# Four layers of multi-query attention: VectorE builds its exps inside their own tile, and the written order of the instructions is replaced

## The chip, the cores and the metric

The kernel runs on one core of a Trainium2 chip. The metric is the device time of one execution in microseconds (us), as the median of several runs. The engines are named as in the profile: PE is TensorE (matmuls), DVE is VectorE, ACT is ScalarE, POOL is GpSimd, SP is SyncE, which here issues the DMAs.

## What is computed

Two sets of weights, A and B, are used in turn for four attention layers over a sequence of 2048 rows of width 512. There are 32 query heads of width 16 and a single key and value head that they all share. Cut to what matters, the reference is:

```python
def layer(x, wq, wk, wv, wo):                # S = 2048, D = 512, H = 32, Dh = 16
    q = (x @ wq).reshape(B, S, H, Dh).transpose(0, 2, 1, 3)
    k = x @ wk
    v = x @ wv
    p = softmax(einsum("bhqd,bkd->bhqk", q, k) * Dh ** -0.5)
    o = einsum("bhqk,bkd->bhqd", p, v)
    return o.transpose(0, 2, 1, 3).reshape(B, S, H * Dh) @ wo

for w in (A, B, A, B):
    x = x + layer(layernorm(x), *w)
```

Each layer has 32 x 2048 x 2048 exponentials, 134 million. They are the bulk of the elementwise work, and they are shared between two engines.

## The kernel before, in words

**Units of work.** A layer is cut into 4 blocks of 512 queries and 4 groups of 8 heads, so there are 16 pairs (block, group) in a layer. For a pair, the 2048 keys are taken in 32 chunks of 64, and each chunk in two *halves*. One half is a tile of scores of 128 partitions x 1024 elements, so there are 4096 halves in the four layers. Each half goes through three steps: PE multiplies queries by keys (the score), one of two engines takes the exp and writes it as float32 into one of 16 slots of the tile `pt`, and PE multiplies the exps by the values and accumulates in `acc`. A column of ones in the value tile gives the sum of the exps in the same matmul, so the division comes at the end of a pair.

**Who takes the exp.** For most halves PE writes the scores into one of two PSUM tiles `st` (function `score`, L746), and ACT reads the whole 128x1024 with one ACTIVATE (L756). For the others PE writes the scores into one PSUM bank, `by_v`, in two parts of 512 (`score_v`, L761), and DVE makes the exp by arithmetic (`exp_first`, L778, and `chain`, L808). That takes eight DVE instructions: two TENSOR_SCALAR (L785), one for each part, scale the score and add a constant, and their int32 output holds the exponent and the fraction of the power of two; one TENSOR_SCALAR (L800) cuts out the fraction into the tile `mant`; one (L802) masks the exponent; three SCALAR_TENSOR_TENSOR (L794) evaluate a polynomial in `mant`; and a fourth (L794 again, reading `e`) multiplies by the exponent's power. The int32 values lie in a tile `e` of which there are two, `e0` and `e1`, taken in turn; the polynomial is evaluated in the slot of `pt` itself. DVE takes its halves 24 halves ahead of ACT (`AHEAD`), so that its longer chain is done when PE needs the exp.

**What else DVE does.** It evacuates every other product from PSUM (queries, keys, values, outputs), does the layer norm, and collects and divides the sums of each pair.

**The other products.** Queries, keys, values and output products of the layers use the PSUM bank `beside`. PE's array is used as two independent halves of 64 rows: a step of the order gives each half of the array one or two groups of four matmuls of 64x32.

**The order.** Nothing schedules at run time or at build time: the string `ORDER` (L55 to L194) is the order of all engines' work, one letter for each step. What matters here: `S` is a score for ACT together with its ACTIVATE; `a` is one value matmul group on each half of the array; `b`, `c`, `d`, `e` put a value group beside product groups; `f` to `k`, `r`, `s` carry a score part for DVE; `P` and `F` are steps that use the whole array; `I` is one L785 of DVE; `0` and `1` are the next instruction of the older and of the younger of at most two DVE chains; `X` is the next DVE step of the products; `G` and `D` evacuate and divide sums; `Y` is a one-element copy (L860) that makes DVE wait for the steps so far; `Q` loads queries by DMA. Each engine runs its instructions in this order, and semaphores hold an instruction until its data are there. PE in particular runs in order: a score that waits holds everything behind it.

**Layer boundaries.** The keys of a new layer come block by block from the outputs of the old one. The new layer's first three pairs take the keys of blocks 0 to 2 first and block 3 afterwards, which gives the last block's chain (output products, layer norm, transposes, key product, the five DVE instructions that begin with `vf`, L578, and end with `kop`, L395) some time. A score that reads block 3's `kop` waits for that chain.

**Waits.** The framework gives each instruction the semaphore waits that its tiles need. When an instruction needs more than one, the others stand before it as instructions of their own (EVENT_SEMAPHORE in the profile). `declare_no_dep` takes a dependence out between two named instructions; it is used where a slot of `pt` is written again, since PE's reads in between order the two writers already.

## Time and profile before

| what | value |
|---|---|
| median of 3 runs | 3555.32 us (3551.79 to 3559.22) |
| the profiled execution's own time | 3529.43 us |
| its span, first to last instruction | 3527.6 us |
| mean granted TensorE clock | 0.994 |
| busy: PE, ACT, DVE | 97%, 97%, 93% of the span |

All durations below come from the profiled execution, which is 25.9 us (0.7%) shorter than the median of the timed runs. In the profile, a group's row gives the instruction's line, engine, operation, output and inputs, the count, the busy time in us and the mean duration in ns, then the idle time of that engine just before them and who ended it. A busy time is the union of the durations. The durations of consecutive instructions on DVE and on ACT overlap, so what an instruction costs its engine is the distance from its start to the next one's start, and not its duration. In the timeline, rows are start, length, engine, line and operation; equal instructions in succession are merged, with `xN` and the length of all.

### The profile page before, as it was taken

How to read it: one execution, taken by the hardware profiler on the slowest of the kernel's cores; microseconds unless marked ns; L12 is line 12 of the kernel's file. 1: busy time of each engine (PE TensorE's matmuls, PEld its weight loads, DVE VectorE, ACT ScalarE, POOL GpSimd, SP SyncE). 2: the span in 40 equal slices, each digit the busy share in tenths (PEclk: the TensorE clock that was granted, in tenths of full speed). 3: DMA queues.
4: the chain of work that ended last, by engine and by line, in shares of the span. 5: the costliest groups of instructions: out<-in, count | busy, mean ns of one | idle time of the engine just before them, and what ended most of it. 6: DMA issues, size and time to landing. Idle time of an engine off the chain costs nothing.

```text
span 3527.6 us, 234143 instructions
## 1 busy us (share of the span) xinstructions
PE 3424.3 (97%) x111859; PEld 2162.8 (61%) x111859; DVE 3288.6 (93%) x4417; ACT 3429.4 (97%) x3728; POOL 158.8 (5%) x110
## 2 busy tenths in 40 slices
PE   7999999999999999999999999999999999999997
PEld 4666666665666666666566666665656666665653
DVE  4869999999989999999998999999999999999994
ACT  6999999999999999999999999999999999999996
POOL 1000001000000000000000010000000010000000
PEclk9999999999999999999999999999999999999999
DMA  2121111111012111011111111101101111111110
GB/s 93 64 74 45 43 42 33 32 40 46 27 43 63 32 43 48 27 49 36 31 31 60 48 45 50 33 31 39 50 23 37 54 43 35 45 34 40 32 33 20
DMA packets 91837, 149.56 MB, mean 42 GB/s; under 512 B 28985, under 2 KB 45369, under 8 KB 90873
## 3 DMA queue, kind: packets, MB, share of 16 engines
q1 hardware_dynamic: 90872, 134.49, 12.0%
q8 instruction: 876, 14.35, 1.6%
q14 instruction: 89, 0.72, 0.1%
HBM read 90.57 MB, written 34.59 MB: 35 GB/s over the span
## 4 chain that ended last, share of the span: by engine, by line
PE 44%; ACT 43%; DVE 11%; DMA 1%; issue 1%; SPq 0%; POOL 0%; DVEq 0%; ACTq 0%; POOLq 0%
ACT pt L756 43%; PE acc L475 23%; PE st L475 12%; PE beside L475 6%; DVE pt L794 5%; DVE e L785 1%; PE by_v L475 1%; DVE mant L800 1%; DVE e L802 1%; PE beside L372 1%; PE beside L512 1%; DMA rec<-rs 0%; DVE sum L877 0%; SPq L913 0%; DMA qt<-qs 0%
## 5 line engine op out<-in xcount | busy, mean ns | idle before, releaser
L756 ACT ACTIVATE pt<-st 128x1024 f32<-128x1024 f32 x3722 | 3425.2, 1118 | 46.0 <-PE st L475 41.2
L475 PE MATMUL acc<-pt,vop 64*32 64x256 f32 x65536 | 2830.9, 377 | 6.1 <-issue 3.7
L475 PE MATMUL st<-qt,kop 64*32 64x512 f16 x29776 | 1654.3, 381 | 55.1 <-ACT pt L756 36.4
L475 PEld LDWEIGHTS acc<-pt,vop 64*32 64x32 f32 x65536 | 1460.8, 106 | 364.7 <-issue 19.3
L475 PEld LDWEIGHTS <-kop 64*32 64x32 f16 x32768 | 771.3, 90 | 806.2 <-issue 514.8
L794 DVE SCALAR_TENSOR_TENSOR pt<-pt,mant 128x1024 f32<-128x1024 f32 x748 | 913.5, 1221 | 3.7
L785 DVE TENSOR_SCALAR e<-by_v 128x512 int32<-128x512 f32 x748 | 514.0, 687 | 61.2 <-PE by_v L475 33.6
L794 DVE SCALAR_TENSOR_TENSOR pt<-pt,e 128x1024 f32<-128x1024 f32 x374 | 458.6, 1226 | 0.8
L475 PE MATMUL beside<-xnT,wq 64*32 64x512 f16 x5952 | 456.8, 376 | 2.0 <-DVE gv L415 1.1
L794 DVE SCALAR_TENSOR_TENSOR pt<-mant 128x1024 f32<-128x1024 f32 x374 | 455.4, 1218 | 0.0
L475 PE MATMUL beside<-wo,ot 64*32 64x512 f16 x5664 | 432.1, 376 | 4.7 <-issue 2.4
L475 PE MATMUL by_v<-qt,kop 64*32 64x512 f16 x2992 | 298.7, 377 | 2.9 <-DVE e L785 1.5
L802 DVE TENSOR_SCALAR e<-e 128x1024 int32<-128x1024 int32 x374 | 256.7, 686 | 3.2
L800 DVE TENSOR_SCALAR mant<-e 128x1024 int32<-128x1024 int32 x374 | 257.4, 688 | 1.0
L475 PEld LDWEIGHTS <-wq 64*32 64x32 f16 x5952 | 172.4, 92 | 49.3 <-issue 7.9
L475 PEld LDWEIGHTS <-ot 64*32 64x32 f16 x5664 | 163.9, 92 | 49.8 <-issue 10.3
L423 POOL TENSOR_TENSOR sq<-qs 128x512 bf16<-128x512 f16 x64 | 107.9, 1686 | 1066.6 <-DVE qs L420 1066.6
L877 DVE COPY sum<-acc 128x512 f32<-128x512 f32 x128 | 84.4, 682 | 39.4 <-PE acc L475 39.0
L475 PE MATMUL beside<-xnT,wkv 64*32 64x512 f16 x1440 | 107.7, 376 | 0.0
L359 POOL TENSOR_TENSOR rstd<-var,nhalf 128x4 f32<-128x4 f32 x16 | 25.9, 1621 | 1126.5 <-DVE var L358 1126.5
L420 DVE TENSOR_SCALAR qs<-beside 128x512 f16<-128x512 f32 x63 | 43.1, 684 | 25.8 <-PE beside L475 13.3
L448 DVE SCALAR_TENSOR_TENSOR xt<-beside,xt 128x512 f32<-128x512 f32 x64 | 43.8, 684 | 12.3 <-PE beside L512 11.1
(105 smaller groups left out, 755.2 us busy)
## 6 DMA issues: line engine op xcount, KB each, us to landing
qt<-qs SPq DMA_DIRECT2D x85, 512.0 KB
qs<-qs SPq DMA_DIRECT2D x256, 64.0 KB
rec<-rs SPq DMA_DIRECT2D x63, 256.0 KB
xs<-xt SPq DMA_DIRECT2D x48, 256.0 KB
xt<-xs SPq DMA_DIRECT2D x48, 256.0 KB
xt<-in_A_x_dram SPq DMA_DIRECT2D x32, 256.0 KB
sum<-sum SPq DMA_DIRECT2D x252, 32.0 KB
out_dram<-xt SPq DMA_DIRECT2D x16, 256.0 KB
```

The costliest lines, as they stand in the source:

```text
L372: PE.transpose(ps[:, c * P:(c + 1) * P], xn[:, c * P:(c + 1) * P], ident)
L420: V.tensor_scalar(qs[:, 0], ps, BIG, -BIG, ALU.min, ALU.max)
L423: G.tensor_tensor(sq, qs[:, 0], qs[:, 0], ALU.mult)
L448: V.scalar_tensor_tensor(x, ps, 1 / VS / WS, x, ALU.mult, ALU.add)
L475: PE.matmul(o[32 * j:32 * j + 32], w[j][h], x[j][h], start=start, stop=stop, skip_group_check=True, tile_position=(64 * r, 32 * j))
L512: PE.matmul(beside, w, x, start=n == 0, stop=n == 3 * NC - 1)
L756: e = A.activation(pts[:, i], st[s], AF.Exp, scale=SCALE / UP / UP).ins
L785: V.tensor_scalar(e[:, 512 * r:512 * r + 512], by_v, SCALE / UP / UP * LOG2E * 2.0 ** 23, LEAD, ALU.mult, ALU.add)
L794: n = V.scalar_tensor_tensor(p, a, c, b, ALU.add, ALU.mult).ins
L800: lambda: V.tensor_scalar(mant.bitcast(I32), e, 0x7FFFFF, 0x3F800000, ALU.bitwise_and, ALU.bitwise_or),
L802: lambda: V.tensor_scalar(e, e, 0x7F800000, None, ALU.bitwise_and),
L877: V.tensor_copy(sums[pr, odd], acc[odd])
```

## The change

Three things change in the code, and the order string is replaced as a whole.

- The two L785 instructions write their int32 values straight into the half's slot of `pt` (seen as int32), and no longer into `e0` or `e1`, which are gone. The exponent is masked there (now L804).
- The polynomial has a tile of its own, `poly0` or `poly1` in turn with `mant0` and `mant1` (now L805 to L807), and only the last instruction (now L799) writes the slot, reading `poly` and the masked exponent from the slot.
- The dependence on the slot's earlier writer is taken out for the two L785 (now L788), which come first in the slot now, and no longer for the first polynomial step.

The number and the shapes of the instructions of one DVE exp stay the same. The new order has 3714 `S` in place of 3722 and 764 `I` in place of 748, so ACT takes 8 halves fewer and DVE 8 more; `P` goes from 72 to 108, which does some products of the first layer on the whole array; the other work is the same in amount. The `1` go from 380 to 467, so two DVE chains are interleaved more often.

```diff
@@ ORDER (140 lines, all replaced; the lines of the second layer boundary)
-    "qcaXaXaaXFXaXaXSGSrGISXsXXSIaaX0Sj0qScIc0SsqqISc0qSaq1SaY0Sbb1Sb0Sba0SaSa0aSQap0SaSa0aSlGpSGppSXarXSaIaS"
+    "SaXa0Sb0Sb0bSbp0Sal0SaSc0cSccScScaYSbpSaXaXSaXSaXaXSQFSXaXXaXXSaSabGSbpSGkppISbhSIpaY0Sc0qSc0qSca0Saq0Sa"
@@
     def exp_first():
         r, new = pend.popleft()
         if new is not None:
-            k = now["e"] = 1 - now["e"]
             assert len(chains) < 2
-            fresh.append((one.tile([P, 1024], I32, name=f"e{k}"), k, new))
-        e, k, n = fresh[-1]
-        V.tensor_scalar(e[:, 512 * r:512 * r + 512], by_v, SCALE / UP / UP * LOG2E * 2.0 ** 23, LEAD,
-                        ALU.mult, ALU.add)
+            fresh.append(new)
+        n = fresh[-1]
+        i = tile_of[n]
+        p = pts[:, i]
+        e = p.bitcast(I32)
+        w = V.tensor_scalar(e[:, 512 * r:512 * r + 512], by_v, SCALE / UP / UP * LOG2E * 2.0 ** 23, LEAD,
+                            ALU.mult, ALU.add).ins
+        if writer[i] is not None:
+            tc.declare_no_dep(w, writer[i], reason="behind the reads in between")
         if new is not None:
             return
-        i = tile_of[n]
-        p = pts[:, i]
+        k = now["e"] = 1 - now["e"]
         mant = one.tile([P, 1024], F32, name=f"mant{k}")
-
-        def write(k, a, c, b):
-            n = V.scalar_tensor_tensor(p, a, c, b, ALU.add, ALU.mult).ins
-            if k == 0 and writer[i] is not None:
-                tc.declare_no_dep(n, writer[i], reason="behind the reads in between")
-            writer[i] = n
+        poly = one.tile([P, 1024], F32, name=f"poly{k}")
+
+        def last():
+            writer[i] = V.scalar_tensor_tensor(p, poly, C0, p, ALU.add, ALU.mult).ins
 
         chains.append(deque([
             lambda: V.tensor_scalar(mant.bitcast(I32), e, 0x7FFFFF, 0x3F800000, ALU.bitwise_and,
                                     ALU.bitwise_or),
             lambda: V.tensor_scalar(e, e, 0x7F800000, None, ALU.bitwise_and),
-            lambda: write(0, mant, C3, mant),
-            lambda: write(1, p, C2, mant),
-            lambda: write(2, p, C1, mant),
-            lambda: write(3, p, C0, e.bitcast(F32))]))
+            lambda: V.scalar_tensor_tensor(poly, mant, C3, mant, ALU.add, ALU.mult),
+            lambda: V.scalar_tensor_tensor(poly, poly, C2, mant, ALU.add, ALU.mult),
+            lambda: V.scalar_tensor_tensor(poly, poly, C1, mant, ALU.add, ALU.mult),
+            last]))
```

How this moves DVE's instructions is shown at two places. The first is an ordinary stretch of the second layer before the change. `pt_85` is the whole tile of 16 slots, `by_v_368` the scores for DVE; a name's last number only tells one use of a buffer from the next, and what stands in brackets are the semaphores that the instruction waits for, named by the engine that counts them up (`DVE_49` is DVE's own).

```order
L794 SCALAR_TENSOR_TENSOR pt_85<-pt_85,mant0_20265 128x1024 [waits DVE_49]
L785 TENSOR_SCALAR e1_20420<-by_v_368 128x512 [waits PE_49]
L794 SCALAR_TENSOR_TENSOR pt_85<-pt_85,e0_20219 128x1024 [waits DVE_49]
L785 TENSOR_SCALAR e0_20646<-by_v_368 128x512 [waits DVE_49,PE_49]
L800 TENSOR_SCALAR mant1_20586<-e1_20420 128x1024
L802 TENSOR_SCALAR e1_20420<-e1_20420 128x1024 [waits DVE_49]
L794 SCALAR_TENSOR_TENSOR pt_85<-mant1_20586 128x1024
L794 SCALAR_TENSOR_TENSOR pt_85<-pt_85,mant1_20586 128x1024 [waits DVE_49]
L785 TENSOR_SCALAR e0_20646<-by_v_368 128x512 [waits PE_49]
```

And this is a stretch of the same part of the program after the change, on the same engine.

```order
L799 SCALAR_TENSOR_TENSOR pt_85<-poly0_19979,pt_85 128x1024 [waits DVE_49]
L788 TENSOR_SCALAR pt_85<-by_v_368 128x512
L802 TENSOR_SCALAR mant1_20237<-pt_85 128x1024 [waits Activation_49]
L804 TENSOR_SCALAR pt_85<-pt_85 128x1024 [waits DVE_49]
L805 SCALAR_TENSOR_TENSOR poly1_20238<-mant1_20237 128x1024
L788 TENSOR_SCALAR pt_85<-by_v_368 128x512 [waits PE_49]
L862 COPY seen_177<-beside_369 128x1 [waits PE_49]
L806 SCALAR_TENSOR_TENSOR poly1_20238<-poly1_20238,mant1_20237 128x1024 [waits DVE_49]
L802 TENSOR_SCALAR mant0_20472<-pt_85 128x1024 [waits DVE_49,Activation_49]
L807 SCALAR_TENSOR_TENSOR poly1_20238<-poly1_20238,mant1_20237 128x1024 [waits DVE_49]
```

Before, the first score of a new chain (the second L785) follows the last instruction of the old chain and has to wait for it, since that instruction still reads `e0`; it waits for PE besides. After, it takes a free slot and waits for PE alone, or for nothing. In its place the fraction (L802) waits for ACT besides DVE, since an ACTIVATE wrote the slot before. In the whole program, 219 of the 748 L785 wait for DVE and PE and 73 for DVE alone; after the change none of the 764 waits for DVE. On ACT it is the other way round: all 3722 ACTIVATEs but the first wait for PE alone before; after, 341 of the 3714 wait for DVE and PE, because DVE has now also read the slot that they write, and only its last writer is declared as no dependence.

The second place is DVE at the boundary between the second and the third layer, from the last instructions of the layer norm's transposes (`xnT`) to the new keys of block 3 (`kop0_3`), before the change.

```order
L794 SCALAR_TENSOR_TENSOR pt_85<-pt_85,e1_48255 128x1024 [waits DVE_49]
L378 CAST xnT0_48274<-beside_369 128x4x128 [waits PE_49]
L380 TENSOR_TENSOR xnT1_48275<-beside_369,xnT0_48274 128x4x128 [waits DVE_49]
L860 COPY seen_177<-beside_369 128x1 [waits PE_49]
L578 TENSOR_SCALAR vf_48841<-beside_369 32x512 [waits PE_49]
L384 STREAM_SHUFFLE tmp_48851<-beside_369 128x512
L388 TENSOR_SCALAR tmp_48851<-tmp_48851 128x512 [waits DVE_49]
L391 CAST kop0_3_105<-tmp_48851 128x512 [waits DVE_49]
L395 SCALAR_TENSOR_TENSOR kop0_3_105<-kop0_3_105,odds_98,tmp_48851 128x512 [waits DVE_49]
```

The same place after the change:

```order
L379 CAST xnT0_47926<-beside_369 128x4x128 [waits PE_49]
L788 TENSOR_SCALAR pt_85<-by_v_368 128x512 [waits PE_49]
L381 TENSOR_TENSOR xnT1_47927<-beside_369,xnT0_47926 128x4x128 [waits DVE_49]
L802 TENSOR_SCALAR mant0_48279<-pt_85 128x1024 [waits DVE_49,Activation_49]
L804 TENSOR_SCALAR pt_85<-pt_85 128x1024 [waits DVE_49]
L805 SCALAR_TENSOR_TENSOR poly0_48280<-mant0_48279 128x1024
L806 SCALAR_TENSOR_TENSOR poly0_48280<-poly0_48280,mant0_48279 128x1024 [waits DVE_49]
L807 SCALAR_TENSOR_TENSOR poly0_48280<-poly0_48280,mant0_48279 128x1024 [waits DVE_49]
L799 SCALAR_TENSOR_TENSOR pt_85<-poly0_48280,pt_85 128x1024 [waits DVE_49]
L862 COPY seen_177<-beside_369 128x1 [waits PE_49]
L579 TENSOR_SCALAR vf_48589<-beside_369 32x512 [waits PE_49]
L385 STREAM_SHUFFLE tmp_48599<-beside_369 128x512
```

A whole chain of DVE now stands between the last transposes and the key product. On PE, the letters say what moved. Counted as steps that PE takes one after the other, with a step of two product groups counted as two, the old order has 17 steps between one `S` and the next at this boundary, and 20 at the boundary between the third and the fourth layer; everywhere else, the first 20 scores aside, it has at most 6. In the old order no `S` stands between the key product and the first score that needs the new keys, at either boundary. In the new order four stand there at the first of the two and eleven at the second, and from the 17th score on no two `S` are more than 6 steps apart.

More of the change, by code (lines that the diff above doesn't have):

```diff
@@ new lines @@
+    "XSXFXaSaXXSXaXXXaSXaXSaXXaXSXaXSXQaaSSaXaXSFGSGlXSamXSXraISFSXaaXSgXSIaaX0SF0SXa0SamXSa0SFSXQa0aSaSXaa0S"
+    "qqqGSqqGcScjSaIqSiISaY0aS0bp0SbpSb0bSb0SaaXSaXSQa0FSaXSXaXaSaXXXSGllXXXSmGSrXXaSIaaXXSaXXSsaXISaX0aS0l0S"
+    "aaXSXS0FSQaXa0SaSaXaXSa0SFGSrGlISaXsSaIaXSaXSX0am0S0FSaXSa0aSaXSa0aSQF0SaaXSaXSappGSppGpSkbISbhSIpaY0Sc0"
+    "qSc0cSc0Sca0SaqSaXaXSa0SQaaXSFXXSaaXXSXaXXSbGbSkGnISbShaISa0a0Sa0Scqq0ScqSc0aSc0SaaSQqaYSbaXSaXSaaSbGpSG"
+    "kpISbhSIb0Sa0bS0aSaYa0Scq0SccS0aScaSQaqScaXSaXSaaSbGpSGkppISahSIbp0Sa0aS0aSc0cScq0SccS0aSaaSQqaYSbaXSaXS"
@@ new lines @@
+    "abGSbpSGkppISbhSIpaY0Sc0qSc0cSc0Saa0ScqSaXa0SaSQaXaSFSXaaXSapSGbShbISpGgSIbb0Sa0Sa0aSa0pSaaY0ScScX0aSaXS"
+    "QaXaDSXaqSaaSmGSGqcSaXmXSaSiDImSjaISa0qSa0SXe0mSaXSaXSaaSQaXXSaDSaXaDS0PPSPGPPGSgDSaIaSDa0rSaIaS0fSaIaS0"
+    "PP0SPD0PPSsaISP0PSaQaXSa0SaaXSaDj0ScqSmGqIScGcSDi0ScIaYSDaDp0Sa0Sab1Skb0SbbD1Sa0Sba1SaaXSa0SaaISaXSaDc0S"
+    "ccDSj0cSaISaDaSDh0bSbISb0b0Skb0SaaYIScD0SiaXSa0SaaXSa0SaaISFDrXSaIScDc0ScDq0Sc0Sic1SaY0Sbb1Sb0Sbb1SbaXSa"
+    "0SaaSIaXSa0jScaISa0jSa1aS0aSbIaS0bs0SaaISQa0Sic1Sc0qScaY1SbGpSp0aSpGpSpIpaXSa0SaaXSaDj0SccISc0Scc1Sqa0Sa"
@@ new lines @@
+    "aY0Sh0SbbISb0kSbaISaD0kSa1Sa0aSaIpSaXa0SaXSaDjqISc0Sic1Sa0qSaa1Sa0Sbb1Sbb0SbSbIaY0SjcSeIaXSa0SaaXSa0rSFI"
+    "SaXaXSbSaaSaXX0aS0kaISa0pSka1Sb0bSaXSa0aScXqXSc0qScIqSaXa0Sa0ShaISQaXp0SkaSaXaY0SaqSGqeXS0mSmGmSIaXSaXaS"
+    "aSalXXSa0rScIc0Sc0jScq1Sa0qSqmY1Sb0ppSpp1pSppp0SppSIaSXaa0SkbISa0Sbb1Sa0aSa0Sc0aSaj0SaaISc0SiaISa0qSiaIS"
+    "c0Sj0qaYISb0pSbaXSa0Sba1Sa0kSbb1Sa0SaaISc0jScIcS0cSc1aS0aqSaY1aS0aSb0hSaaIS0bSaaXSsXXaISaXaXSDQaXXSaDaSX"
+    "XarDSXa0aSaX1SlGSGmD0SaaISaXSXa0aS0FSaXa0SaSaXaXSaDSa0aSFD0SaSXaaDSaXsSXaIaSXD0FS0aXrSaISaXa0SFSXsaISaXg"
@@ L194 @@
+    "aSSaaSSaaSSaaSSaaSSaaSSaaaaGGDDDDDDDDDDDDDDDDDDDDDDDDPPPPPPPPPPPPXPPPPPPPPPPPPXPPPPPPPPPPPPXPPPPPPPPPPPP"
+    "XX"
 )
```

258 lines of the change are left out of this document (121 added, 137 removed).

## The prediction

> **What bounds the kernel now.** I read the page first, then who waits for whom on ACT and on PE, then the windows of 200 us, and at last the timelines.
>
> ```profile
> span 3527.6 us, 234143 instructions
> PE 3424.3 (97%) x111859; PEld 2162.8 (61%) x111859; DVE 3288.6 (93%) x4417; ACT 3429.4 (97%) x3728; POOL 158.8 (5%) x110
> ...
> PE 44%; ACT 43%; DVE 11%; DMA 1%; issue 1%; SPq 0%; POOL 0%; DVEq 0%; ACTq 0%; POOLq 0%
> ...
> L756 ACT ACTIVATE pt<-st 128x1024 f32<-128x1024 f32 x3722 | 3425.2, 1118 | 46.0 <-PE st L475 41.2
> ```
>
> PE and ACT are both busy for 97%. PE's matmuls overlap and their ends are modelled, so its share says little; the waits say more.
>
> ```profile
> ACT pt L756 <- PE st L475: 41.2, 44, 7.7
> ```
>
> ```profile
> PE st L475 <- ACT pt L756: 36.4, 94, 0.7
> ```
>
> The columns are the total in us, the times, and the longest. PE waits for ACT 94 times, never above 0.7 us: it stands at a score until ACT has emptied a buffer. ACT waits 44 times, but with few long ones. So ACT is the bound nearly everywhere, and PE only at a few places. An exp costs 3425.2 / 3722 = 0.920 us of ACT. These are the places of the long waits:
>
> ```profile
> 31.69 1.94 ACT L756 ACTIVATE pt<-st 128x1024 f32<-128x1024 f32 x2 [7.74 <-PE st L475]
> 34.87 1.02 ACT L756 ACTIVATE pt<-st 128x1024 f32<-128x1024 f32 x1 [1.25 <-PE st L475]
> 36.63 12.02 ACT L756 ACTIVATE pt<-st 128x1024 f32<-128x1024 f32 x13 [0.73 <-PE st L475]
> 51.87 8.36 ACT L756 ACTIVATE pt<-st 128x1024 f32<-128x1024 f32 x9 [3.22 <-PE st L475]
> ...
> 1884.51 7.54 ACT L756 ACTIVATE pt<-st 128x1024 f32<-128x1024 f32 x8
> 1896.28 9.28 ACT L756 ACTIVATE pt<-st 128x1024 f32<-128x1024 f32 x10 [4.23 <-PE st L475]
> ...
> 2744.40 9.39 ACT L756 ACTIVATE pt<-st 128x1024 f32<-128x1024 f32 x10
> 2758.64 7.45 ACT L756 ACTIVATE pt<-st 128x1024 f32<-128x1024 f32 x8 [4.85 <-PE st L475]
> ```
>
> Four waits (12.9 us) lie in the first 52 us, where the first keys and queries are made. The other two long ones, 4.23 and 4.85 us, lie exactly at the two layer boundaries where the old order has 17 and 20 steps of PE without a score. The remaining 41.2 - 12.9 - 9.1 = 19.2 us are spread over 38 waits.
>
> The second engine without room is DVE:
>
> ```profile
> core 0: us, PE busy (x) PEld busy (x) DVE busy (x) ACT busy (x) POOL busy (x), PEclk, DMA share, GB/s
> ...
> 1400.00:1600.00 200.00, 198.69 (x6586) 127.68 (x6578) 195.83 (x258) 199.82 (x219) 10.62 (x6) 1.00 0.12 38
> 1600.00:1800.00 200.00, 194.33 (x6364) 122.11 (x6353) 196.70 (x261) 199.30 (x219) 4.68 (x2) 1.00 0.11 34
> ...
> 3200.00:3400.00 200.00, 191.83 (x6222) 118.41 (x6209) 193.94 (x235) 198.96 (x218) 0.00 (x0) 1.00 0.11 33
> ```
>
> In most windows DVE is busy for 194 to 197 of 200 us beside ACT's 199. The order has dealt the exps so that both end together; giving DVE more work is free only if it loses as much elsewhere.
>
> **Part 1: eight exps leave ACT.** 3722 - 3714 = 8 exps at 0.920 us are 7.4 us off ACT's path. The range of this term is small: at the best cadence of the windows, 200 / 219 = 0.913 us, it is 7.3.
>
> **Part 2: eight chains more on DVE, and the waits that go.** What an instruction costs DVE is the distance between starts:
>
> ```profile
> 1806.42 1.22 DVE L794 SCALAR_TENSOR_TENSOR pt<-mant 128x1024 f32<-128x1024 f32 x1
> 1807.56 1.22 DVE L794 SCALAR_TENSOR_TENSOR pt<-pt,e 128x1024 f32<-128x1024 f32 x1
> 1808.88 0.69 DVE L785 TENSOR_SCALAR e<-by_v 128x512 int32<-128x512 f32 x1
> 1809.49 1.22 DVE L794 SCALAR_TENSOR_TENSOR pt<-pt,mant 128x1024 f32<-128x1024 f32 x1
> ...
> 1820.77 0.68 DVE L800 TENSOR_SCALAR mant<-e 128x1024 int32<-128x1024 int32 x1
> 1821.37 1.22 DVE L794 SCALAR_TENSOR_TENSOR pt<-pt,mant 128x1024 f32<-128x1024 f32 x1
> 1822.51 0.68 DVE L802 TENSOR_SCALAR e<-e 128x1024 int32<-128x1024 int32 x1
> 1823.11 1.22 DVE L794 SCALAR_TENSOR_TENSOR pt<-pt,e 128x1024 f32<-128x1024 f32 x1
> ...
> 1824.97 1.22 DVE L794 SCALAR_TENSOR_TENSOR pt<-mant 128x1024 f32<-128x1024 f32 x1
> 1826.22 2.49 DVE L794 SCALAR_TENSOR_TENSOR pt<-pt,mant 128x1024 f32<-128x1024 f32 x2
> ```
>
> An L785 takes 0.61 us (1808.88 to 1809.49), L800 and L802 0.60 each, an L794 1.14 (1806.42 to 1807.56, or 1821.37 to 1822.51). A chain is 2 x 0.61 + 2 x 0.60 + 4 x 1.14 = 6.98 us, eight of them 55.8 us. Against that stands the wait that the diff removes. An L794 followed by an instruction that needs its result takes 1.25 us (1824.97 to 1826.22); one followed by an L785 that waits for it, and for PE through a separate wait instruction, takes 1.32 us (1807.56 to 1808.88).
>
> ```profile
> L785 DVE TENSOR_SCALAR e<-by_v x748: 671/690/693, 99.7 to 3456.7; 128x512 int32<-128x512 f32 x187
> L785 DVEq EVENT_SEMAPHORE  x219: 21/21/21, 276.3 to 3454.9; - x110
> ```
>
> These 219 waits give back up to 219 x 0.18 = 39 us. The 73 that wait for DVE alone give at most 73 x 0.11 = 8 us. The new order also has fewer steps of one chain right behind each other (66 polynomial pairs instead of 130, by the order): 64 x 0.11 = 7 us. Sum for DVE: +55.8 - 39 - 8 - 7 = +2 us. I cost it at nothing: DVE has 239 us of idle time in all, though in the dense windows its cover is only 3 to 6 us of 200, so if the waits stayed, the 55.8 us would be on the path (a rival below). The new fraction step (now L802) waits for DVE and ACT at 255 places; the ACT part is met long before, since PE has read that slot since, and behind it only its own chain and the next evacuation are queued. The first L788 of a half needs a free slot earlier than the polynomial did, at no cost: the slot is taken from the free ones when PE makes the score, behind PE's reads of it.
>
> [...]
>
> **Part 3: the two boundaries.** The new order has no stretch of more than 6 steps of PE without a score there, and four and eleven scores stand between the key product and the first score that needs the new keys. What has to fit under them is DVE's work on the keys:
>
> ```profile
> 1892.70 0.68 DVE L578 TENSOR_SCALAR vf<-beside 32x512 f32<-32x512 f32 x1 [3.25 <-PE beside L475]
> ...
> 1894.99 0.75 DVE L395 SCALAR_TENSOR_TENSOR kop<-kop,odds,tmp 128x512 f16<-128x512 f16 x1
> ```
>
> From 1892.70 to 1894.99 + 0.75 = 1895.74 it is 3.04 us, and four exps are 4 x 0.92 = 3.7 us of ACT's work. It fits, narrowly at the first boundary. So both waits go: 4.23 + 4.85 = 9.1 us. What is late next there is ACT itself. Bounds: 0 (the waits come back as a wait on the keys) to 9.1.
>
> **Part 4: the second wait on 341 exps of ACT.** No row of ACT shows an exp that waits for two engines. The nearest rows are DVE's. Where the extra waits were met before, they cost almost nothing:
>
> ```profile
> L927 DVEq EVENT_SEMAPHORE  x126: 21/50/2190, 243.4 to 3456.6; - x126
> L927 DVE TENSOR_TENSOR sum<-sum,rec x63: 673/683/930, 244.0 to 3457.3; 128x512 f32<-128x512 f32 x63
> its engine sat idle before it (us, times) until:
>   issue: 1.1, 3
> ```
>
> 126 extra waits before 63 instructions left 1.1 us of idle time, 9 ns each: the wait instruction is worked off while the instruction before it still runs. Where it was not met in time, it cost 1.32 - 1.25 = 0.07 us above the plain wait. On ACT the awaited DVE instruction belongs to the slot's former exp, which PE has read in the meantime, so it is always met; I take 0. The upper end is 341 x 0.07 = 24 us; a gain is excluded, as nothing is taken away. [...]
>
> **The sum.** 7.4 + 9.1 = 16.5 us, with 0 for DVE and 0 for the second waits. Against the profiled execution: 3529.4 - 16.5 = 3512.9 us. The timed runs lie 25.9 us above it, and I carry that over: 3555.3 - 16.5 = 3538.8 us. The chances count from 0.2%, 7.1 us, about what a measurement of this kernel can tell from no change.
>
> **The rivals.**
> 1. *The gain is spent on new waits* (no change). A new order has new places where PE comes late; the old one has 19.2 us of scattered waits after all planning. If the keys' wait comes back at the first boundary and some 5 to 10 us of new ones are added, 16.5 shrinks to 2 to 7: 3548 to 3553 us. For it: only 3.7 us cover 3.04 us, and the product work is denser behind the boundaries. Against it: eleven scores at the other boundary. Chance 0.14.
> 2. *The second wait is not hidden on ACT* (slower). Place: 341 exps on the engine that sets the end, about one in eleven. Price: 0.07 us each is 24 us, 3538.8 + 24 = 3563 us; it decides from 16.5 / 341 = 0.048 us each. For it: ACT is the bound and has no room. Against it: the L927 rows, and ACT's exps start 0.92 us apart at a mean length of 1.118 us, so the next one is made ready while one runs. Chance 0.08.
> 3. *DVE becomes the bound* (slower). If the 1.32 us stays, some 47 of the 55.8 us remain; about 12 of the 17 full windows are dense like those shown, and 47 x 12 / 17 = 33 us come on the path: 3538.8 + 33 = 3572 us. Against it: the order shows no DVE wait left on the L788. [...] Chance 0.05.
> 4. *More is gained.* The scattered 19.2 us fall as well, since DVE's results come earlier: up to 3538.8 - 19.2 = 3519.6 us. Chance 0.13.
>
> That the change doesn't do what it says is excluded for its waits by the order.
>
> **How the numbers follow.** The forecast has 0.60, the rivals 0.14, 0.08, 0.05 and 0.13. The likeliest case alone is 3531 to 3546 us (part 3 between 4 and 9.1, and some scattered waits less). The range goes to half of rival 4 below and through rival 1 and the lower half of rival 2 above: 3524 to 3557 us. Faster by over 0.2% (below 3548.2 us) holds the forecast and rival 4: 0.73. The same: rival 1, 0.14. Slower: rivals 2 and 3, 0.13.
>
> **What would show it.** Right: ACT's row with x3714 at 0.920 us each; no wait of 4 us on ACT after the first 52 us; an L799 followed by an L788 1.14 us apart; DVE still at 194 to 197 us in the dense windows. Wrong: starts of exps behind a wait instruction more than 0.95 us apart (rival 2); waits of PE's value matmuls on `pt` from DVE (rival 3); new rows of ACT waiting for `st` of over a microsecond (rival 1).

## The result, and the profile after

The changed kernel takes 3582.35 us (median of 6 runs, 3579.18 to 3592.17), the kernel before 3553.56 us in the same comparison (6 runs, 3548.20 to 3559.22). The ratio is 1.0086, 95% interval 1.0069 to 1.0103: slower by 28.8 us, where 16.5 us less were forecast. The profiled execution's own time is 3582.92 us.

First the page of the kernel after: span, busy times, and the group of ACT's exps with ACT's idle time before them.

```profile
span 3581.1 us, 234086 instructions
...
PE 3440.9 (96%) x111607; PEld 2226.5 (62%) x111607; DVE 3325.5 (93%) x4480; ACT 3453.5 (96%) x3720; POOL 153.4 (4%) x110
...
L757 ACT ACTIVATE pt<-st 128x1024 f32<-128x1024 f32 x3714 | 3449.2, 1074 | 74.1 <-PE st L476 63.1
```

Then who waits for whom on ACT and on PE (total in us, times, longest).

```profile
ACT pt L757 <- PE st L476: 63.1, 125, 8.1
...
PE st L476 <- ACT pt L757: 45.1, 126, 0.5
...
PE acc L476 <- issue: 11.7, 24, 1.3
PE beside L476 <- issue: 5.2, 8, 1.7
PE st L476 <- issue: 4.7, 15, 0.9
...
PE acc L476 <- DVE pt L799: 0.4, 2, 0.2
```

ACT waits for PE's scores 125 times where it waited 44 times, and for 63.1 us in place of 41.2. That is only part of the loss. ACT's busy time grew as well, from 3425.2 to 3449.2 us, although there are 8 exps fewer: an exp lasts 1.074 us on average and the next one starts some 0.91 us after it (median 0.912 us), so an exp that comes late by less than this overlap leaves no idle time. Of the 53.5 us between the two spans, 28.1 us are idle time of ACT (46.0 to 74.1) and 24.0 us are busy time. The long waits have gone: after the first 55 us none is above 1.92 us, and the waits of 4.23 and 4.85 us at the two layer boundaries are not there any more. In their place stand many short ones. PE never waits for VectorE's exps (0.4 us), so VectorE has not become the bound. And there are waits of PE for "issue": time in which PE waited for nothing that the profile shows.

The windows say where. Here are three of the kernel after, engine by engine with the number of instructions; ACT's number is that of its exps.

```profile
700.00:900.00 200.00, 194.01 (x6306) 124.55 (x6293) 198.07 (x261) 199.46 (x218) 4.11 (x2) 1.00 0.11 34
...
1100.00:1300.00 200.00, 196.27 (x6654) 137.82 (x6641) 189.51 (x256) 193.00 (x206) 15.10 (x9) 1.00 0.16 46
...
1700.00:1900.00 200.00, 191.95 (x6256) 121.91 (x6248) 196.05 (x255) 198.08 (x215) 3.27 (x2) 1.00 0.10 29
```

Late in a layer, where few products are left, ACT takes 215 to 218 exps in 200 us. At the beginning of a layer, 1100 to 1300 us, it takes 206. These are the matmuls of the other products (tile `beside`) in such windows, of the kernel after:

```profile
700.00:900.00 200.00, 38.50 (x500) 1.00 0.11 34
...
1100.00:1300.00 200.00, 88.35 (x1142) 1.00 0.16 46
...
1900.00:2100.00 200.00, 91.50 (x1182) 1.00 0.18 53
```

The time is lost where PE has most to do. But the amount of work does not explain it: these are the same two views of the kernel before, first the engines and then the product matmuls, in its window with the most of them. It had 1106 there and still gave ACT 219 exps. (The kernel e8 below has 1263 in that window, and 217 exps.)

```profile
1900.00:2100.00 200.00, 199.93 (x6792) 127.94 (x6793) 194.30 (x252) 199.85 (x219) 18.21 (x11) 1.00 0.16 51
```

```profile
1900.00:2100.00 200.00, 83.09 (x1106) 1.00 0.16 51
```

What happens in such a stretch is seen in the timeline. ACT, in the kernel after, 276 to 293 us:

```profile
276.75 3.77 ACT L757 ACTIVATE pt<-st 128x1024 f32<-128x1024 f32 x4 [0.31 <-PE st L476]
280.71 4.05 ACT L757 ACTIVATE pt<-st 128x1024 f32<-128x1024 f32 x4 [0.18 <-PE st L476]
285.03 4.10 ACT L757 ACTIVATE pt<-st 128x1024 f32<-128x1024 f32 x4 [0.27 <-PE st L476]
289.74 2.86 ACT L757 ACTIVATE pt<-st 128x1024 f32<-128x1024 f32 x3 [0.62 <-PE st L476]
```

And PE in the same stretch, only the rows that end an "issue" wait:

```profile
275.83 0.42 PE L476 MATMUL acc<-pt,vop 64*32 64x256 f32 x4 [0.18 <-issue]
...
284.12 0.44 PE L476 MATMUL acc<-pt,vop 64*32 64x256 f32 x6 [0.42 <-issue]
...
288.40 0.87 PE L476 MATMUL acc<-pt,vop 64*32 64x256 f32 x22 [0.39 <-issue]
```

Four exps, a wait, four exps, a wait: one about every 4 us, each 0.9 to 1.3 us behind a standstill of PE. The wait at 280.71 us has its standstill too: for 0.51 us, up to 279.84 us, no instruction of PE starts, but matmuls that had begun earlier still run, so their rows show no idle time. The page's part on DMA queues shows what has that rhythm, a packet of queue 8 for every 4.1 us of the span (3581.1 / 874). It lists packets, MB, and the share of 16 engines' span:

```profile
q1 hardware_dynamic: 90872, 134.49, 12.2%
q8 instruction: 874, 14.32, 1.7%
```

Queue 8, which the page names "instruction", keeps step with PE's own instructions. Its 874 packets are 16 KB each, and 874 x 256 = 223,744, which is the number of PE's matmuls and weight loads (2 x 111,607 = 223,214) and a few more: a block of 256 instructions for each packet. In the kernel before (876 packets) and in e8, e9 and e10 below (774, 793 and 934) the packets times 256 exceed PE's matmuls and weight loads by only 354 to 538 too. I counted in the trace where PE's starts lie more than 0.26 us apart with no semaphore awaited (they usually lie at most 0.22 us apart; what exceeds 0.215 us is counted as the standstill), between 60 and 3500 us, and where that standstill ends 0.8 to 1.65 us after the end of a queue-8 packet. There are 136 in the kernel after, 44.8 us in all, and 126 of them end at a record whose number leaves 188 or 189 when divided by 256: the seam of two blocks. One packet begins for each seam: the packets begun and the seams passed so far agree in number at 855 of the 856 seams between 60 and 3500 us. At the 136 standstills, in the median, PE's last start comes 2.08 us after the packet's transfer has begun, the transfer takes 1.16 us (1.10 us over all packets), and PE goes on 1.39 us after its end. The next start is then 0.46 us behind the last one, in place of at most 0.22 us. The seams themselves say the same. At 130 of the 856 seams in this stretch the starts lie more than 0.26 us apart, and at 128 of these the time from the start of the last transfer to PE's arrival at the seam was shorter than that transfer plus 1.39 us; of the 726 others, 196 were short of it.

Most seams show nothing, 726 of the 856; but with 136 standstills, 44.8 us in all, the crossing is not hidden where PE comes early.

### The profile page after: what moved, and what is told of

It reads as the page before. It is cut to its first block, busy times and chain, and to the rows that moved or that the text cites. A ratio compares the mean times of both kernels' runs of the same rounds, so it can differ in the third digit from the quotient of the medians.

```text
span 3581.1 us, 234086 instructions
## 1 busy us (share of the span) xinstructions
PE 3440.9 (96%) x111607; PEld 2226.5 (62%) x111607; DVE 3325.5 (93%) x4480; ACT 3453.5 (96%) x3720; POOL 153.4 (4%) x110
## 5 line engine op out<-in xcount | busy, mean ns | idle before, releaser
L757 ACT ACTIVATE pt<-st 128x1024 f32<-128x1024 f32 x3714 | 3449.2, 1074 | 74.1 <-PE st L476 63.1
L476 PE MATMUL acc<-pt,vop 64*32 64x256 f32 x65536 | 2910.7, 376 | 15.1 <-issue 11.7
L476 PE MATMUL st<-qt,kop 64*32 64x512 f16 x29712 | 1823.6, 380 | 79.6 <-ACT pt L757 45.1
L476 PEld LDWEIGHTS acc<-pt,vop 64*32 64x32 f32 x65536 | 1579.6, 106 | 393.5 <-issue 51.4
L476 PEld LDWEIGHTS <-kop 64*32 64x32 f16 x32768 | 797.5, 90 | 751.5 <-issue 484.2
L788 DVE TENSOR_SCALAR pt<-by_v 128x512 int32<-128x512 f32 x764 | 525.1, 687 | 64.8 <-PE by_v L476 49.5
L807 DVE SCALAR_TENSOR_TENSOR poly<-poly,mant 128x1024 f32<-128x1024 f32 x382 | 468.6, 1227 | 0.6
L799 DVE SCALAR_TENSOR_TENSOR pt<-poly,pt 128x1024 f32<-128x1024 f32 x382 | 468.4, 1226 | 0.4
L806 DVE SCALAR_TENSOR_TENSOR poly<-poly,mant 128x1024 f32<-128x1024 f32 x382 | 467.0, 1222 | 1.3
L805 DVE SCALAR_TENSOR_TENSOR poly<-mant 128x1024 f32<-128x1024 f32 x382 | 466.1, 1220 | 0.0
L804 DVE TENSOR_SCALAR pt<-pt 128x1024 int32<-128x1024 int32 x382 | 263.2, 689 | 2.3
L802 DVE TENSOR_SCALAR mant<-pt 128x1024 int32<-128x1024 int32 x382 | 263.2, 689 | 1.4
L476 PEld LDWEIGHTS <-wq 64*32 64x32 f16 x5760 | 177.5, 92 | 61.3 <-issue 20.8
```

Source lines behind the costliest of these rows:

```text
L476: PE.matmul(o[32 * j:32 * j + 32], w[j][h], x[j][h], start=start, stop=stop, skip_group_check=True, tile_position=(64 * r, 32 * j))
L757: e = A.activation(pts[:, i], st[s], AF.Exp, scale=SCALE / UP / UP).ins
L788: w = V.tensor_scalar(e[:, 512 * r:512 * r + 512], by_v, SCALE / UP / UP * LOG2E * 2.0 ** 23, LEAD, ALU.mult, ALU.add).ins
L799: writer[i] = V.scalar_tensor_tensor(p, poly, C0, p, ALU.add, ALU.mult).ins
L802: lambda: V.tensor_scalar(mant.bitcast(I32), e, 0x7FFFFF, 0x3F800000, ALU.bitwise_and, ALU.bitwise_or),
L804: lambda: V.tensor_scalar(e, e, 0x7F800000, None, ALU.bitwise_and),
```

## The experiments

The theory: the new order lets PE run through more seams without a pause, and PE's instruction supply has become the limit there (**supply**). The rivals: PE's work lies worse in the new order whatever the supply (**order**), or the tile edit with its second waits on ACT is to blame (**tiles**). The table sums up what the traces show. A late exp starts more than 0.96 us after the one before; counted is what it starts beyond 0.915 us, apart for exps within 2.5 us behind a standstill at a seam and for the others, between 60 and 3500 us. "Again" marks a second execution of the same program.

| execution | span | median transfer of a block | standstills at seams | late exps behind one | other late exps |
|---|---|---|---|---|---|
| before, as first shown | 3527.6 | 0.958 us | 34, 12.4 us | 19.5 us | 39.3 us |
| before, again | 3554.5 | 1.075 | 78, 27.6 | 41.3 | 47.1 |
| old order, new tiles | 3547.6 | 1.093 | 71, 24.7 | 37.8 | 41.9 |
| after | 3581.1 | 1.099 | 136, 44.8 | 66.3 | 51.9 |
| new order, old tiles | 3594.0 | 1.102 | 133, 41.1 | 65.3 | 70.7 |
| before, more weight loads | 3664.3 | 1.047 | 288, 109.7 | 143.7 | 54.6 |
| after, joined | 3508.6 | 1.039 | | 6.3 | 42.6 |
| after, joined, again | 3506.9 | 0.974 | | 5.2 | 40.6 |
| old order, new tiles, joined | 3513.6 | 0.991 | | 6.4 | 35.8 |
| before, joined | 3527.7 | 0.973 | | 10.8 | 47.6 |

(In the joined kernels, matmuls of 512 columns are by themselves over 0.26 us apart (0.428 us from step to step in e8), so standstills can't be counted by that rule. Their late exps are counted behind every place that the rule finds, so the numbers behind a seam are upper values.)

**The order or the tiles.** e1_old_order is the kernel after with the string `ORDER` of before; e2_old_tiles is the kernel before with the string of after.

```diff
-ORDER = (...)   # of after
+ORDER = (...)   # of before
```

> The old order with the new tiles (VectorE's scores go into the slot of their exp, the exponent is masked there, the polynomial has its own tile). Three theories of the 28.8 us by which the change is slower. Order: the new order lays PE's steps so that scores come late at the layer starts; then this kernel has none of the loss, and less of the waits that VectorE had: 3540 to 3554 us. Instruction supply: PE's instructions come in blocks of 16 KB, and PE stands still at the seam of two blocks more often in the new order, because there it runs longer without waiting for ACT; the same 3540 to 3554 us, with as few standstills without a wait as before (79 above 0.26 us between 60 and 3500 us, against 185 after). Tiles: the second wait on some 340 exps and the longer hold of the slots are to blame; then 3575 us or more.

> The new order with the old tiles (scores into a tile of their own, polynomial in the slot). Order and instruction supply: the loss stays, and some waits of VectorE for its own results come back: 3580 to 3600 us. Tiles: 3555 us or less, since ACT's second waits are gone.

Measured: 3546.95 us for e1, ratio to before 0.9998 (0.9989 to 1.0008), and 3592.01 us for e2, ratio 1.0122 (1.0105 to 1.0139). The order alone makes the loss. The tiles alone are worth nothing with the old order. With the new order they are worth something: 1.0122 against 1.0086 for after is 0.36%, some 13 us. The two ratios come from separate comparisons and their intervals only just lie apart, but the spans in the table differ by 12.9 us as well, and it is the other late exps that differ (70.7 against 51.9 us). In e2 PE waits for VectorE to free `by_v`, which in the kernel after takes 1.6 us in 3 waits. The rows are those of VectorE's line that reads `by_v` (L786 in e2): its wait instructions, and who waited for it (us, times).

```profile
L786 DVEq EVENT_SEMAPHORE  x234: 21/21/21, 263.9 to 3521.3; - x117
...
  PE by_v L476: 13.0, 30
```

So the new order needs the new tiles. The theory "tiles" falls.

**The kernel before, once more.**

> The kernel before once more, for its trace: the profiled execution shown first was 25 us faster than the timed ones. If that was a matter of how long the blocks of PE's instructions take to come (median 0.958 us there, 1.10 us in the trace of after), this execution lies at 3550 to 3558 us and has a median above 1.0 us; if the length of a fetch belongs to the program and has no part in it, the median is 0.96 us again, whatever the span.

Measured: 3548.72 us, ratio 0.9999 (0.9989 to 1.0009), and the profiled execution has a span of 3554.5 us, 26.9 us more than the one shown first, with the same program and the same clock (0.994). Two windows of it:

```profile
1100.00:1300.00 200.00, 198.86 (x6677) 129.62 (x6661) 195.81 (x249) 198.29 (x216) 16.97 (x9) 1.00 0.15 41
1300.00:1500.00 200.00, 197.00 (x6454) 125.77 (x6460) 192.76 (x257) 196.13 (x212) 10.60 (x6) 1.00 0.13 39
```

And the second of them in the execution shown first:

```profile
1300.00:1500.00 200.00, 197.32 (x6580) 125.80 (x6561) 195.60 (x259) 198.23 (x216) 10.62 (x6) 1.00 0.12 38
```

From 1300 to 1500 us it has 212 exps, where the first execution had 216; from 1100 to 1300 us both have 216. By the table its transfers took 0.12 us longer in the median, and 22 of its 27 us are late exps behind seams. The length of a transfer does not belong to the program alone; it differs between these two executions of one program (0.958 and 1.075 us), and here the kernel's time moved with it (3527.6 and 3554.5 us). This is seen on one pair of executions. At nearly equal transfers (1.075 and 1.099 us), before again and after differ by 25.0 us behind seams and by 4.8 us elsewhere.

**Fewer instructions for the same work.** In e8_adj the two halves of a value product (256 columns each) are one matmul of 512 columns, but only where they follow each other directly in the order (`WIDE` holds these places). e9_adj_old is the same edit on e1. Of the edit, these are the lines that matter:

```diff
+        if k - n in WIDE[odd]:
+            x = [pts[:, i[j % 2], (j // 2) * 512:(j // 2) * 512 + 512] for j in range(4)]
+            return None if n else (("acc", odd), acc[odd], [v] * 4, x, c == 2 * c0, c == 2 * c1 - 1)
         return ("acc", odd), acc[odd][:, cs], [v] * 4, x, (c, n) == (2 * c0, 0), last
```

> The changed kernel, in which the two halves of a value product are one matmul of 512 columns only where they follow each other directly in the order (1589 of 4096 pairs for each kind): the slots of PE and their places stay as they are, all matmuls keep their width of 32, and 25,400 of 223,200 PE instructions go. Instruction supply: a block of 256 lasts 13% longer, so most late blocks go (136 standstills at a fetch's end in the trace of after), and with them the 30 us of late exps behind them by which after differs from before: 3540 to 3560 us, and lower if the gain that was forecast shows. Order: PE's slots at the layer starts are too many whatever the supply, 3575 us or more.

> The old order with the new tiles, and the halves of value products joined where they follow each other directly (1321 pairs, 21,100 PE instructions fewer). Instruction supply: the old order's own late blocks (71 to 78 standstills at a fetch's end, some 40 us of late exps behind them) go for the most part: 3515 to 3535 us, the level of the one execution with short fetches (3529 us). Order: no change, 3545 to 3550 us.

Measured: 3512.82 us for e8, ratio to before 0.9907 (0.9894 to 0.9921), and 3517.02 us for e9, 0.9920 (0.9906 to 0.9933). The joined matmuls do the work no faster: a step of eight follows the one before after 0.428 us, and two plain steps take 2 x 0.216 us. By the ratios, an edit that leaves PE's work and its places as they are takes 1.8%, 64 us, off the changed kernel (1.0086 to 0.9907) and 0.8%, 28 us, off its twin with the old order (0.9998 to 0.9920). Both are faster than the kernel before. Lines of the page of e8, and one window:

```profile
q8 instruction: 774, 12.68, 1.5%
...
L774 ACT ACTIVATE pt<-st 128x1024 f32<-128x1024 f32 x3714 | 3424.6, 1081 | 26.5 <-PE st L492 21.9
```

```profile
1100.00:1300.00 200.00, 199.62 (x6263) 133.08 (x6257) 197.94 (x271) 199.61 (x217) 14.07 (x8) 1.00 0.17 51
```

A hundred blocks fewer, ACT's waits down from 63.1 to 21.9 us, and 217 exps in the window that had 206. The "issue" time before the weight loads of the value products falls with it; these are the groups of weight loads, first of after, then of e8 (the larger "issue" time before the scores' weight loads does not go with the seams: it is 514.8 us before, 484.2 after and 688.0 in e8):

```profile
L476 PEld LDWEIGHTS acc<-pt,vop 64*32 64x32 f32 x65536 | 1579.6, 106 | 393.5 <-issue 51.4 <-DVE pt L799 3.7 <-DVE sum L879 3.5
```

```profile
L492 PEld LDWEIGHTS acc<-pt,vop 64*32 64x32 f32 x52824 | 1291.0, 106 | 280.5 <-DVE sum L903 9.4 <-issue 8.0 <-DVE pt L816 5.4
```

This is the theory's case against "order": late exps behind seams fall to 6 us in both orders, by 60 us in the new one (66.3 to 6.3) and by 31 us in the old one (37.8 to 6.4), and the others fall by only 9 and 6 us. A count that also serves for the joined kernels says the same. PE's starts lie more than 0.26 us apart at 130 of 856 seams after and at 7 of 767 in e8, at 69 of 864 in e1 and at 12 of 786 in e9. PE reaches a seam 2.67 us after the start of the last transfer in the kernel after and 3.42 us after it in e8 (medians). A transfer of 1.04 us and the 1.39 us that passed behind it at the standstills are 2.43 us, so by this estimate the block is there in time at most seams of e8.

The transfers were quicker as well in these traces (1.039 against 1.099 us, and 0.991 against 1.093 us), which may be a part of the falls; the ratios are each taken to the kernel before in the same comparison, which ran at 3547.8 us for e8 and e9 and at 3547.7 us for e1. e8 came out below its range of 3540 to 3560 us, which its expectation allowed if the gain that was forecast showed; e9 lies inside its range.

**More instructions for the same work.** e10_more adds four weight loads behind every score to the kernel before, which no matmul uses.

```diff
+        for r in range(2):
+            for j in range(2):
+                PE.ldweights(moving(n, r)[0][j][64 * r:64 * r + 64], tile_position=(64 * r, 32 * j))
```

> The kernel before with four more weight loads behind every score that no matmul uses (14,900 PE instructions more, 6.7%; PE's weight loads are busy for 61% of the span beside the matmuls). Instruction supply: blocks are used up faster, standstills and late exps rise at least to those of after: 3575 to 3650 us. Order: the loads lie beside matmuls, 3545 to 3560 us.

Measured: 3662.65 us, ratio 1.0324 (1.0307 to 1.0341), above the range given. ACT's and PE's waits:

```profile
ACT pt L759 <- PE st L475: 115.8, 203, 8.0
...
PE acc L475 <- issue: 24.4, 53, 1.7
PE st L475 <- issue: 21.5, 36, 1.9
PE beside L475 <- issue: 10.7, 24, 1.2
```

288 standstills at seams, 143.7 us of late exps behind them, and 54.6 us elsewhere, hardly more than before. The old order gets the loss, and far more of it, by its number of instructions. A little of the 114 us may be the loads' own time: the "other" late exps rise by 7.5 us over those of the second execution of before, and 11.3 us of ACT's waits (22 of them) are put down to the new loads.

**Other ways to save instructions, which did not decide.** e3_wide joins all the halves of value products, also where a score lies between them. e5_few gives a score two matmuls of 64 columns for each half of the array, in place of four of 32; e6_few_old does this with e1, and e7_fewer also takes the products in matmuls of 128 columns. These are the lines of e5 that change the score:

```diff
-        return (cols(k) * 2, [q[:, 2 * h], q[:, 2 * h], q[:, 2 * h + 1], q[:, 2 * h + 1]], True, True)
+        return ([k] * 2, [q[:, 2 * h], q[:, 2 * h + 1]], True, True)
```

> The changed kernel, with the two halves of each value product (256 columns each) issued as one matmul of 512 columns: the same work for PE in 65536 instructions fewer (some 158,000 instead of 223,000). Instruction supply: a block of 256 then lasts PE over 5 us, no block comes late, and the time falls to 3550 us or below, with fewer than 60 standstills without a wait. Order: PE's work stays where it is and becomes lumpier (four slots in one piece), so 3582 us or more.

> The changed kernel (new order, new tiles), with every score issued as two matmuls of 64 columns for a half of the array instead of four of 32: the same products in the same places, some 33,000 PE instructions fewer (190,000 instead of 223,000), so that a block of 256 instructions lasts five exps instead of 4.3. Instruction supply: PE hardly stands still at the seams any more (fewer than 60 standstills at the end of a fetch, 136 in the trace of after), its work fits as it was laid out, and the gain that was forecast shows: 3515 to 3540 us. Order: the work of PE as such is too dense at the layer starts; nothing changes, 3575 us or more. A third possibility is that matmuls of two widths don't run beside each other; then it is far slower, over 3600 us, and tells nothing of the two.

> The old order with the new tiles, and the scores as two matmuls of 64 columns. Instruction supply: the old order has fewer late blocks to lose (71 standstills at a fetch's end, 25 us), so it gains less than the new order does: 3520 to 3535 us, about the 3529 us of the one execution of before in which the fetches were short. Order: no change, 3547 us.

> As e5, and the products of queries, keys and outputs as one matmul of 128 columns for a half of the array instead of four: 171,000 PE instructions. Instruction supply: as e5 or a few us less, 3510 to 3540 us, because the last seams go from the stretches with many products. Order: as after, 3575 us or more. If matmuls that take the whole width have to wait for the narrow ones beside them, it is slower than e5 by more than 10 us.

Measured: e3 3631.32 us (ratio 1.0235, 1.0218 to 1.0252). By its time it lies in the range of "order" (3582 us or more) and not in that of "supply". It has the fewest blocks of the kernels with 32 columns (618), but PE's work comes in larger lumps, and a score that lay between two halves now comes behind both: PE waits for ACT 302 times, 95.4 us, and ACT for PE 98 times, so each waits for the other. Its late exps behind seams come to 25.4 us at most, where the kernel after has 66.3, and the other ones to 144.0 us, where it has 51.9. So the loss at the seams is smaller in e3 too, but the edit moves PE's work and brings a new loss of its own. It does not decide. e5 took 4435.93 us (1.2503, 1.2483 to 1.2524), e6 4473.02 us (1.2611, 1.2590 to 1.2632), e7 5238.86 us (1.4768, 1.4743 to 1.4792). The timeline of PE in e5 shows why:

```profile
1500.06 0.40 PE L477 MATMUL acc<-pt,vop 64*32 64x256 f32 x4
1500.25 0.39 PE L477 MATMUL beside<-xnT,wq 64*32 64x512 f16 x4
1500.28 0.40 PE L477 MATMUL acc<-pt,vop 64*32 64x256 f32 x4
1500.60 0.41 PE L477 MATMUL st<-qt,kop 64*64 64x512 f16 x4
1500.94 0.61 PE L477 MATMUL beside<-xnT,wq 64*32 64x512 f16 x8
```

Value groups follow each other at 0.22 us (1500.06 to 1500.28). From the last of them to the score it is 0.32 us, and from the score to the next group 0.34 us: each change of width costs 0.1 us or a little more. Over the whole trace the medians are 0.306 us for a score behind a group of 32 columns and 0.330 us for a group behind a score, with some 2890 of each; two groups of 64 columns follow each other at 0.230 us. By an estimate from these distances, two changes for each of 3714 scores at 0.10 to 0.12 us are 740 to 890 us, and e5 is 854 us above the kernel after. So e5 is far slower, as in the third possibility of its expectation, and e7 is 803 us above e5, as in that of its own. That matmuls of two widths can't run beside each other, or that wide ones wait for the narrow ones, was not shown; what the trace of e5 shows is the 0.1 us at each change.

**What the change is worth when instructions are not the limit.** e11_adj_before is the kernel before with the joined halves; e12_adj_again is e8 once more, beside it.

> The kernel before (old order, old tiles) with the halves of value products joined where they follow each other directly (1321 pairs). Instruction supply: as its twin with the new tiles, 3515 to 3525 us, since what both lose at the seams of the instruction blocks is gone. Beside the joined form of the changed kernel it shows what the change is worth when PE's instructions are not the limit: the forecast's 16.5 us would put it at 3526 to 3532 us; if new waits had eaten the gain whatever the supply, it lies no higher than the joined changed kernel, at 3513 us or below.

> The joined changed kernel again, on the chip and beside the runs of the joined kernel before, for a direct comparison: 3510 to 3515 us, as in its first runs.

Measured: e11 3521.79 us, ratio to before 0.9966 (0.9953 to 0.9979); e12 3513.35 us, 0.9940 (0.9927 to 0.9953). The kernel before itself ran at 3535.63 us in this comparison, 10 to 18 us less than in the others; the transfers took 0.97 us in both traces. By the medians the joined changed kernel is 8.4 us faster than the joined kernel before, by the means 11.4 us; their runs spread over 6.3 and 11.8 us, so the size is only roughly known. ACT's waits, of e11 and of e12:

```profile
ACT pt L773 <- PE st L491: 39.9, 46, 8.1
```

```profile
ACT pt L774 <- PE st L492: 18.9, 23, 7.4
```

46 waits become 23. The profiled execution of e11 was the slowest of its six and that of e12 the quickest of its five, 20.8 us apart, so these totals show more than the medians do. What does not hang on that are the two boundary waits. e11 has both, in these rows of ACT's timeline:

```profile
1901.15 9.27 ACT L773 ACTIVATE pt<-st 128x1024 f32<-128x1024 f32 x10 [4.22 <-PE st L491]
...
2762.54 8.36 ACT L773 ACTIVATE pt<-st 128x1024 f32<-128x1024 f32 x9 [4.83 <-PE st L491]
```

At the same two places e12 has 28 and 34 exps in a row without a wait. So 9.05 us of waits that the forecast counted on losing are lost here. The gain is half of the 16.5 us forecast by the medians, and two thirds by the means.

## Why the prediction was wrong

- *Part 1, eight exps at 0.920 us:* the eight exps went, but the price did not hold. An exp costs 3449.2 / 3714 = 0.929 us after, which is 33 us more for 3714 of them: the late exps within the overlap. In e8 it is 0.922 us.
- *Part 2, VectorE at no cost:* right. The last step of a chain and the next evacuation are 1.14 us apart, as the timeline of DVE in the kernel after shows; over the whole trace the median of 292 such places is 1.135 us, and in e2, where the waits are back, it is 1.32 us at 231 places. PE waits for VectorE's exps for 0.4 us only. What the terms of the sum for VectorE (39, 8 and 7 us) came to one by one was not measured. e1 puts the tiles at 0.9998. With the new order the removed waits are needed: without them (e2) it is some 13 us slower.

```profile
1805.41 1.23 DVE L799 SCALAR_TENSOR_TENSOR pt<-poly,pt 128x1024 f32<-128x1024 f32 x1
1806.55 0.69 DVE L788 TENSOR_SCALAR pt<-by_v 128x512 int32<-128x512 f32 x1
1807.15 1.22 DVE L805 SCALAR_TENSOR_TENSOR poly<-mant 128x1024 f32<-128x1024 f32 x1
```

- *Part 3, the two boundary waits:* right; both are gone, in the kernel after and in e12, while e11 with the old order has them.
- *Part 4, the second wait on ACT:* right. There are 342 wait instructions in the trace, the exps behind them start 0.920 us after the exp before, and all the other exps 0.949 us. Those means hold the late exps; by the medians it is 0.920 against 0.912 us, and 0.909 against 0.907 us in e8. So a wait costs 0.01 us at most, 3 us in all, where rival 2 priced it at 0.07 us. Rival 2 falls.
- *The sum:* here it failed. It took what the forecast does not name as unchanged: "The remaining 41.2 - 12.9 - 9.1 = 19.2 us are spread over 38 waits", and PE as late "only at a few places". So it put new lateness of PE at nothing, and PE came late at 136 seams of instruction blocks, with 66.3 us of late exps behind them. The first rival had the outside of it, new scattered waits with denser product work, but not the cause, and priced it at 5 to 10 us, against 16.5 us of gain. The terms that were counted come to 8.4 us of gain by the medians where supply is hardly a limit (e12 against e11), and what was not counted took 28.8 + 8.4 = 37 us. Joining takes 64 us off the new order and 28 us off the old one, a difference of 36 us, which agrees.
- *The carry-over of 25.9 us* from the profiled execution to the timed ones was added as a constant. It was no constant: the execution that all the rows came from had quick transfers, 0.958 us against 1.075 us, and few standstills (34). The price of a seam was in that trace, 12.4 us, but it was not looked for, since the waits named "issue" came to no more than 3.7, 2.4 and 1.2 us in PE's three rows there.

What stays open: why the new order brings PE to so many seams too early. More product matmuls at the layer starts go with it (nine windows of 200 us with over 900 of them hold 110 of its standstills), but the old order has a window with 1085 of them and 3 standstills. Nor is it known why a transfer takes 0.96 us in one execution and 1.08 us in another. It may belong to the chip. The later comparisons ran on three chips, and the medians of their traces are 1.06 to 1.10 us in the seven of the first (e1, e2, e3, e5, e6, e7 and before again), 0.99 to 1.05 us in the three of the second (e8 to e10), and 0.97 us in both of the third (e11 and e12). Which chip the execution shown first ran on is not known. One program on two chips, traced several times on each, was not tried.

## What to carry to other kernels

This fully written-out kernel, which keeps TensorE busy with small matmuls, was also limited by how fast its instructions arrive (136 standstills at seams, 66.3 us of late exps). In another such kernel, compare the number of instructions for one step of the bounding engine with the blocks of 256 that come in that time (here a block for 4.3 exps, 3.9 us, on average; at the seams where PE stood, PE went on 2.5 us after the last transfer had begun, and its last start before that came after 2.1 us). Waits put down to "issue" at even distances were its sign here. A tenth fewer instructions for the same work were worth more than the new order. ACT's exps overlap, 1.074 us long and 0.912 us apart, and the lateness hid in its busy time, which grew by 24.0 us with eight exps fewer, so look at the distances between starts as well as at its waits. Before the gap between a profiled and a timed execution is carried over as a constant, look for what moves it.

## What the runs showed of the hardware

- Where PE stood at a seam in the kernel after, it went on 1.39 us (median) after the end of the last queue-8 transfer, and that transfer had begun 2.08 us before PE's last start. Nine in ten transfers took 0.9 to 1.4 us. By an estimate from its densest steps, PE uses up a block of 256 in some 3.45 us: sixteen steps of eight 64x32 matmuls and their eight weight loads, 0.215 to 0.216 us each.
- The same program's transfers took 0.958 us in one execution and 1.075 us in another, and the span went from 3527.6 to 3554.5 us. Over the other traces the median goes with the chip: 1.06 to 1.10, 0.99 to 1.05 and 0.97 us on three of them.
- A change between matmuls of 32 and of 64 columns costs some 0.1 us here: the next group starts 0.31 to 0.33 us after the last, where groups of one width follow at 0.22 to 0.23 us. e5, with two changes for each score, takes 25% longer.
- A wait instruction that is already met costs ACT at most 0.01 us: from start to start it is 0.920 us behind one and 0.912 us elsewhere in the kernel after, 0.909 and 0.907 us in e8 (medians).
- An L794 of 128x1024 in the kernel before holds VectorE for 1.32 us where the L785 behind it waits for VectorE and PE and so has a wait instruction ahead of it. In the kernel after, where no L788 waits for VectorE, an L799 with an L788 behind it holds VectorE for 1.14 us (medians of 210 places before and 292 after).
- A matmul of 512 columns in float32 does the work of two of 256 with half the instructions and in the same time (0.428 us a step against 2 x 0.216 us); joined where they adjoin, the changed kernel is the fastest of the forms run: 0.9907 and 0.9940 of the kernel before in two comparisons.
